# Expert 0's first layer on its first 256 rows moved among the last batch's routing, expert 1's first 256 rows in a pass of their own, column clears on GpSimd

## The chip, the cores and the metric

The kernel runs on one core of a Trainium2 chip, in one launch. The metric is the device time of that launch in microseconds (us): the median of several executions. One further execution, recorded by the hardware profiler, gives the trace from which rows are shown.

The engines are called as the profile calls them: PE is TensorE (matmuls; its weight loads are PEld), DVE is VectorE, ACT is ScalarE, POOL is GpSimd, SP is SyncE, which here only issues transfers.

## The reference

Three stages follow each other. All data are float32.

```python
# attention: 4 batches x 8 heads, 768 steps, heads of 48
for t in range(S):
    state = alpha[:, :, t, :, None] * state + einsum('bhd,bhe->bhde', k[:, :, t], v[:, :, t])
    y[:, :, t] = einsum('bhd,bhde->bhe', q[:, :, t], state)
# mixture of experts: N = 3072 rows of 384, 8 experts, hidden 1024, one expert per row
logits = (x / |x|) @ (emb / |emb|).T / tau
expert_idx = argmax(logits); gate_w = softmax(logits)[expert_idx]
out[mask_e] = gate_w * (relu(x[mask_e] @ w1[e]) @ w2[e])      # for each expert e
# a second feed-forward layer on all rows, hidden 2048
h = x @ w_in;  g = maximum(0.01 * h, h);  return g @ w_out
```

A row's expert is known only when its attention output is complete, so the experts' work starts after the routing.

## The kernel before, in words

**Precision.** A float32 product is made of three float16 matmuls: each operand is split into a high part and the rest (names end in h and l), and high x high, low x high and high x low are summed in one PSUM bank.

**Attention** runs over 16 units, four pairs of heads in each of four batches. Its operations are handed to `Plan` with an estimated duration, what they read and write, which PSUM bank they use, and a wish time `plan.at`. `Plan.order` makes a list schedule out of these, and the program is written in that order, one in-order queue for each engine. Where the plan expects gaps on PE, `keep_busy` puts matmuls without use (`pfill`, L357) into them.

**Routing.** `route(b)` follows each batch b: norms, logits, the arg max, the rank of each row within its expert (`ranks`) and its slot. Six indirect transfers on POOL (`scatter`, L667, one for each 128 rows) then write the rows of the batch, with their gate weight, into `bucket`, a table in DRAM with one region for each expert. Each scatter of a batch is issued behind the last.

**Early rows.** Of each expert's region the static part is CAP = 432 rows. `early_rows` fetches the first E0 = 256 rows of expert 0 (SP, L682, two blocks) once batch 2 is scattered, while the last batch is routed: these rows are the same whatever batch 3 adds. ACT scales them (L689), PE transposes them (L686), ACT writes the high part (L691) and DVE the rest (L692) of `xte`, which lies in the tile `shared`.

**The expert stage.** Its own `Plan` orders it. For expert e, `up(e, f, ...)` makes the eighth f of the hidden layer (9 matmuls: 3 products x 3 pieces of the contraction), with the relu into `held` by ACT (L1099) and the rest by DVE (L1100). `down(e, d, ...)` makes one third of the output columns (24 matmuls, L1118 to L1120), read by ACT (L1129) and DVE (L1130) into the column tiles `x2h` and `x2l`. Before the change, expert 0's `up` and `down` on the early 256 rows come first (f at wish times from -40, d from -30), then the rest of expert 0 (176 columns), then each expert with 432. Four PSUM banks `ps1` and four `ps2` are used in turn.

**Around it.** The weights of expert 0 are converted to float16 pairs during attention; those of expert e + 1, and pieces of the second layer's weights, during expert e (`fetch`, L1043; `piece`, L1048 on ACT and L1049 on DVE). Expert 1's tiles lie over tiles of the attention stage. `gather` fetches the other rows of experts 0 and 1 from `bucket` after the last scatter. `clear` (L1139) writes zeros on the columns behind each expert's static part, 12 pieces of 128 x 660, on ACT. After the routing the totals are counted by one matmul (L811) whose result gives the offsets of the experts, and `few`, which tells whether expert 0 had fewer than 256 rows after batch 2 (in which case a general pass at the end does its rows again).

The second feed-forward layer (L881 to L917) is PE work alone in its cost and is not touched, except that its weight pieces are spread otherwise over the experts.

## Time and profile before

| | |
|---|---|
| median of 3 runs | 738.17 us (738.13 to 738.73) |
| the profiled execution | 738.29 us |
| its span in the trace | 736.5 us |
| busy in the span: PE, DVE, ACT, POOL | 712.5, 583.4, 387.2, 100.6 us |
| mean granted clock of TensorE | 0.99 |

The span runs from the first to the last recorded instruction; the launch has 1.8 us around it. Busy shares are means over stages with different limits: attention and routing take the first 158 us or so, the experts and the second layer the rest, and a share tells nothing of which wait ends last in one stage. Granted clock 1.00 is TensorE's level of 2.4 GHz, 0.50 that of 1.2 GHz.

### The profile page before, as it was taken

To read this page: it belongs to the slowest core of one execution; us is meant where nothing else is said; L and a number is where in the kernel's file an instruction comes from. 1 tells how busy PE (TensorE), PEld (TensorE's weight loads), DVE (VectorE), ACT (ScalarE), POOL (GpSimd) and SP (SyncE) were. 2 spreads that over 40 slices of the span, in tenths; PEclk is the share of its full clock that TensorE was granted. 3 is DMA by queue.
4 is the path that set the end of the run, shared out by engine and by line. 5 is a ranking of instruction groups with operands and counts; after the bars stand their busy time and mean duration, and the time that the engine had idled before them with its cause. 6 is when DMAs were issued, how large, how long until landed. Compare 5 with 4: busy or idle time off the path is not lost.

```text
span 736.5 us, 16493 instructions
## 1 busy us (share of the span) xinstructions
PE 712.5 (97%) x6683; PEld 556.5 (76%) x6683; DVE 583.4 (79%) x1115; ACT 387.2 (53%) x758; POOL 100.6 (14%) x125
## 2 busy tenths in 40 slices
PE   7999989789999999999999999999999999999997
PEld 3778767558655555555588777999999999999996
DVE  7889889558887879988988888877878778768681
ACT  3354636339976677766755454443544544435440
POOL 7433635330000000000000110011010010110101
PEclk9999989899999999999999999999999999999999
DMA  8987935418999689886400000000000000000001
GB/s 297 304 239 234 293 128 172 142 66 189 269 251 239 196 196 236 200 232 181 144 1 1 13 16 19 1 23 22 2 22 2 23 24 1 23 23 2 24 1 46
DMA packets 62544, 82.77 MB, mean 112 GB/s; under 512 B 30840, under 2 KB 42496, under 8 KB 62464
## 3 DMA queue, kind: packets, MB, share of 16 engines
q1 hardware_dynamic: 58080, 71.13, 35.4%
q0 software_dynamic: 4224, 10.53, 4.0%
q8 instruction: 54, 0.88, 0.5%
q14 instruction: 26, 0.21, 0.1%
q10 hardware_dynamic: 160, 0.01, 0.0%
HBM read 62.09 MB, written 12.12 MB: 101 GB/s over the span
## 4 chain that ended last, share of the span: by engine, by line
PE 86%; DMA 5%; DVE 4%; ACT 1%; POOL 1%; issue 1%; another core or an unknown queue 1%; SPq 0%; POOLq 0%; DVEq 0%; ACTq 0%
PE ps L881 9%; PE ps L883 9%; PE ps L882 9%; PE ps L917 6%; PE ps L916 6%; PE ps L915 6%; PE ps L1094 5%; PE ps L1092 5%; PE ps L1093 5%; PE ps L1120 5%; PE ps L1119 5%; PE ps L1118 5%; PE py L516 2%; PE psc L456 2%; PE py L475 2%; DMA q<-in_qT 1%
## 5 line engine op out<-in xcount | busy, mean ns | idle before, releaser
L881 PE MATMUL ps<-x2h,wih 128*128 128x256 f16 x576 | 157.0, 273 | 0.0
L882 PE MATMUL ps<-x2l,wih 128*128 128x256 f16 x576 | 157.0, 273 | 0.0
L883 PE MATMUL ps<-x2h,wil 128*128 128x256 f16 x576 | 157.0, 273 | 0.0
L889 DVE TENSOR_TENSOR held<-ps,held 128x512 f32<-128x512 f32 x96 | 65.9, 686 | 51.0 <-ACT held L888 50.9
L949 POOL DMA_INDIRECT out<-wstage,tki x24 | 25.5, 1061 | 540.5 <-ACT wstage L1256 283.7
L888 ACT ACTIVATE held<-ps 128x512 f32<-128x512 f32 x96 | 57.3, 597 | 78.0 <-PE ps L883 61.6
L1118 PE MATMUL ps<-held,w2h 128*128 128x432 f16 (+2 forms) x216 | 70.1, 326 | 0.0
L1119 PE MATMUL ps<-held,w2h 128*128 128x432 f16 (+2 forms) x216 | 70.1, 326 | 0.0
L1120 PE MATMUL ps<-held,w2l 128*128 128x432 f16 (+2 forms) x216 | 70.1, 326 | 0.0
L1093 PE MATMUL ps<-xt,w1h 128*128 128x432 f16 (+1 forms) x192 | 63.6, 333 | 0.5 <-DVE xt L1018 0.5
L1092 PE MATMUL ps<-xt,w1h 128*128 128x432 f16 (+1 forms) x192 | 63.6, 333 | 0.4 <-ACT xt L1017 0.4
L1094 PE MATMUL ps<-xt,w1l 128*128 128x432 f16 (+1 forms) x192 | 63.6, 333 | 0.0
L881 PEld LDWEIGHTS <-wih 128*128 128x128 f16 x576 | 56.4, 98 | 6.8
L882 PEld LDWEIGHTS <-wih 128*128 128x128 f16 x576 | 56.4, 98 | 6.7
L883 PEld LDWEIGHTS <-wil 128*128 128x128 f16 x576 | 56.4, 98 | 6.5
L1100 DVE SCALAR_TENSOR_TENSOR held<-ps,held 128x432 f16<-128x432 f32 (+2 forms) x72 | 39.0, 552 | 11.8 <-ACT held L1099 9.8
L1099 ACT ACTIVATE held<-ps 128x432 f16<-128x432 f32 (+2 forms) x72 | 34.8, 488 | 23.9 <-PE ps L1094 23.4
L928 DVE SCALAR_TENSOR_TENSOR wstage<-ps,ms,wstage 128x192 f32<-128x192 f32 x80 | 31.9, 411 | 16.8 <-PE ps L917 16.7
L900 ACT ACTIVATE o1h<-held 128x256 f16<-128x256 f32 (+1 forms) x40 | 20.9, 523 | 30.7 <-DVE held L889 30.0
L900 ACT ACTIVATE o0h<-held 128x256 f16<-128x256 f32 (+1 forms) x40 | 20.9, 523 | 30.3 <-DVE held L889 29.7
L461 DVE TENSOR_TENSOR am<-psc,mask 128x768 f32<-128x768 f32 x32 | 30.0, 938 | 6.9 <-remote 3.7
L667 POOL DMA_INDIRECT bucket<-xb,slot x24 | 30.9, 1289 | 32.4 <-ACT shared L691 15.9
(282 smaller groups left out, 1869.6 us busy)
## 6 DMA issues: line engine op xcount, KB each, us to landing
wstage<-in_w SPq DMA_DIRECT2D x64, 384.0 KB
wstage<-in_w_in SPq DMA_DIRECT2D x16, 384.0 KB
wstage<-in_w_out SPq DMA_DIRECT2D x16, 384.0 KB
a<-in_aT SPq DMA_DIRECT2D x12, 387.5 KB
k<-in_kT SPq DMA_DIRECT2D x12, 384.0 KB
q<-in_qT SPq DMA_DIRECT2D x12, 384.0 KB
v<-in_v SPq DMA_DIRECT2D x8, 576.0 KB
xg<-bucket SPq DMA_DIRECT2D x6, 582.0 KB
```

The costliest lines, as they stand in the source:

```text
L881: nc.tensor.matmul(d, wih[:, k, fs], xs[0][k], start=k == 0, stop=False)
L882: nc.tensor.matmul(d, wih[:, k, fs], xs[1][k], start=False, stop=False)
L883: nc.tensor.matmul(d, wil[:, k, fs], xs[0][k], start=False, stop=k == KD - 1)
L888: add("ACT", 0.59, lambda: nc.scalar.activation(dst, src, AF.Copy, scale=0.01), [key], [("g", i)])
L889: add("DVE", 0.69, lambda: nc.vector.tensor_tensor(dst, src, dst, op=ALU.max), [key, ("g", i)], [("g", i)])
L915: nc.tensor.matmul(d, oh, wh, start=k == 0, stop=False)
L1092: nc.tensor.matmul(ps, w1h[:, f, k], xt[:, k], start=k == 0, stop=False)
L1093: nc.tensor.matmul(ps, w1h[:, f, k], xt[:, KD + k], start=False, stop=False)
L1094: nc.tensor.matmul(ps, w1l[:, f, k], xt[:, k], start=False, stop=k == KD - 1)
L1118: nc.tensor.matmul(ps, w2h[:, f, ds_], hh, start=f == 0, stop=False)
L1119: nc.tensor.matmul(ps, w2h[:, f, ds_], hl, start=False, stop=False)
L1120: nc.tensor.matmul(ps, w2l[:, f, ds_], hh, start=False, stop=f == NF1 - 1)
```

## The change

Four things are changed.

1. `early_rows(0)` asks for the row fetch after two of batch 2's scatters instead of six and transposes into the attention stage's banks `pkv` and `py`. A new `early_up` makes all of expert 0's first layer on the 256 rows within the attention plan, at wish time NU + 1.8, in three banks: `pkv` and the two halves of `py`, which is one tile. Its matmuls are L707 to L709, its relu L713 on ACT, its rest L714 on DVE. Fewer filler matmuls stand in that part of the program, and the call of `keep_busy` in `values` is left out.
2. `early_rows(1)` does the same fetch, scaling and transposing for expert 1's first 256 rows, into a weight stage tile. In the expert stage expert 0's `down` now comes first, then expert 1's `up` on those 256 columns, then the rest of expert 0; expert 1's later `up` has 176 columns. Four pieces of expert 1's first weight are fetched ahead of all others.
3. The 12 clears become memsets on POOL.
4. The pieces of the second layer's weights are spread 4, 3, 3, 3, 4, 5, 5, 5 over the experts instead of evenly, and some wish times move. `few` and the count are kept for two experts.

```diff
-        def early_rows():
-
-            u = (RU - 3) % 3
+        def early_rows(e):
+
+            u = (RU - 3 + e) % 3
             rows = (ta[u][:, :AUG], tq[u][:, :AUG])
             scaled = (ta[u][:, AUG:AUG + D], tk[u][:, :D])
             for n in range(E0 // P):
                 ts = slice(n * P, (n + 1) * P)
-                hi, lo = xte[:, :KD, ts], xte[:, KD:, ts]
                 held = ("a", "q")[n], u
-
-                def fetch(n=n, ts=ts):
-                    nc.sync.dma_start(rows[n], bucket[ts])
-
-                def turn(n=n):
+                bank, tp = (f"t{n}", ptr[n].rearrange("p k t -> p (k t)")) if e else (("kv", pkv), ("y0", py[:, 0]))[n]
+                own = ("tr", n) if e else ("eb", bank)
+                tp = tp[:, :KD * P].rearrange("p (k t) -> p k t", k=KD)
+
+                def fetch(n=n):
+                    nc.sync.dma_start(rows[n], bucket[e * NT + n * P:e * NT + (n + 1) * P])
+
+                def turn(n=n, tp=tp):
                     for k in range(KD):
-                        nc.tensor.transpose(ptr[n][:, k], scaled[n][:, k * P:(k + 1) * P], ident)
-
-                plan.add(Q_, 0.45, fetch, [("bucket", B - 2, c) for c in range(NC)], [held], size=(P * AUG * 4, 2.5))
-                plan.add(S_, 0.62, lambda n=n: nc.scalar.activation(scaled[n], rows[n][:, :D], AF.Copy, scale=rows[n][:, D:D + 1]), [held], [("early", n)] + [("k", u)] * n)
-                plan.add(T_, 0.45, turn, [("early", n)], [("tr", n)], pe=[f"t{n}"], flow=2 * KD * P)
-                plan.add(S_, 0.47, lambda n=n, hi=hi: nc.scalar.activation(hi, ptr[n][:, :KD], AF.Copy), [("tr", n)], [("xte", n)], ps=[f"t{n}"])
-                plan.add(V, 0.56, lambda n=n, hi=hi, lo=lo: nc.vector.scalar_tensor_tensor(lo, ptr[n][:, :KD], 1.0, hi, op0=ALU.mult, op1=ALU.subtract),
-                         [("tr", n), ("xte", n)], [("xtl", n)], ps=[f"t{n}"])
+                        nc.tensor.transpose(tp[:, k], scaled[n][:, k * P:(k + 1) * P], ident)
+
+                plan.add(Q_, 0.45, fetch, [("bucket", B - 2, c) for c in range(2)], [held], size=(P * AUG * 4, 1.0))
+                plan.add(S_, 0.62, lambda n=n: nc.scalar.activation(scaled[n], rows[n][:, :D], AF.Copy, scale=rows[n][:, D:D + 1]), [held], [("early", e, n)] + [("k", u)] * n)
+                plan.add(T_, 0.45, turn, [("early", e, n)], [own], pe=[bank], flow=2 * KD * P)
+                plan.add(S_, 0.47, lambda ts=ts, tp=tp: nc.scalar.activation(columns_of(e)[:, :KD, ts], tp, AF.Copy), [own], [("xte", e, n)] + [("wst", 0)] * e, ps=[bank])
+                plan.add(V, 0.56, lambda ts=ts, tp=tp: nc.vector.scalar_tensor_tensor(columns_of(e)[:, KD:, ts], tp, 1.0, columns_of(e)[:, :KD, ts], op0=ALU.mult, op1=ALU.subtract),
+                         [own, ("xte", e, n)], [("xtl", e, n)], ps=[bank])
+
+        def early_up():
+
+            (w1h, w1l), xt = shaped(w_first)[:2], columns_of(0)
+            late_rows = [(x, n, u, j) for x in ("pkh", "pqh") for n in range(2) for u in range(NR) for j in range(2)] + [("pen", 0, u, j) for u in range(NR) for j in range(2)]
+            y = [(f"y{i}", py[:, i]) for i in range(2)]
+            banks = [y[1], ("kv", pkv), y[0]] * 2 + [y[1], y[0]]
+            for f in range(NF1):
+                bank, ps = banks[f]
+                ps = ps[:, :E0]
+                hh, hl = (x[f][:, :E0] for x in hid)
+
+                def go(k, f=f, ps=ps):
+                    nc.tensor.matmul(ps, w1h[:, f, k], xt[:, k], start=k == 0, stop=False)
+                    nc.tensor.matmul(ps, w1h[:, f, k], xt[:, KD + k], start=False, stop=False)
+                    nc.tensor.matmul(ps, w1l[:, f, k], xt[:, k], start=False, stop=k == KD - 1)
+
+                for k in range(KD):
+                    plan.add(T_, 0.33, lambda k=k, go=go: go(k), [(x, f // 2) for x in ("whi", "wlo")] + [(x, 0, n) for x in ("xte", "xtl") for n in range(E0 // P)], [("eb", bank)], pe=[bank], flow=3 * E0)
+                plan.add(S_, 0.37, lambda ps=ps, hh=hh: nc.scalar.activation(hh, ps, AF.Relu), [("eb", bank)], [("hh", f)] + (late_rows if f > 2 else []), ps=[bank])
+                plan.add(V, 0.42, lambda ps=ps, hh=hh, hl=hl: nc.vector.scalar_tensor_tensor(hl, ps, 0.0, hh, op0=ALU.max, op1=ALU.subtract), [("eb", bank), ("hh", f)], [("hl", f)], ps=[bank])
...
+        first = []
+
+        def columns_of(e):
+
+            if e and not first:
+                first.append(stage())
+            return (first[0] if e else shared).bitcast(F16).rearrange("p (k t) -> p k t", k=2 * KD)
...
-            plan.at = NU + 1.7
-            early_rows()
+            plan.at = NU + 1.4
+            early_rows(0)
+            plan.at = NU + 1.8
+            early_up()
+            plan.at = NU + 1.9
+            early_rows(1)
...
+        turns = [1, 2, 3, 1]
+
         def fetch(src, at, cast=None):
-            m = len(fetched) % len(stages)
+            m = turns[len(fetched)] if len(fetched) < len(turns) else (len(fetched) - 2) % len(stages)
...
-                    plan.add(S_, 0.16 + w / 1200, lambda x=x: nc.scalar.activation(x, row0[:, 0:1].to_broadcast([P, w]), AF.Copy), ["bucket"], [("clear", n, d)], at=at)
+                    plan.add(G_, 1.0, lambda x=x: nc.gpsimd.memset(x, 0.0), ["bucket"], [("clear", n, d)], at=at)
...
-        plan.add("WAIT", 10.8, lambda: None, [], ["bucket"])
+        plan.add("WAIT", 8.0, lambda: None, [], ["bucket"])
         second = second_pieces()
-        per = -(-len(second) // E)
+        counts = (4, 3, 3, 3, 4, 5, 5, 5)
+        assert sum(counts) >= len(second)
         def pieces_of(e):
-            mine = [(begin(e) + 4.0 + 2.9 * j, weights, e + 1, j) for j in range(2 * KD * F1 // CH if e + 1 < E else 0)]
-            mine += [(begin(e) + 5.0 + 5.8 * j, *second[e * per + j]) for j in range(min(per, len(second) - e * per))]
+            mine = [(begin(e) + 4.0 + 2.9 * j - 8.0 * (1 <= e < 4), weights, e + 1, j) for j in range(2 * KD * F1 // CH if e + 1 < E else 0)]
...
+        mine = pieces_of(0)
+        add(mine[:4])
+        for d in range(KD):
+            down(0, d, d - 40.0, slice(0, E0))
         for f in range(NF1):
-            up(0, f, xte, f - 40.0, slice(0, E0), True)
-        for d in range(KD):
-            down(0, d, d - 30.0, slice(0, E0), True)
-        mine = pieces_of(0)
-        add(mine[:6])
+            up(1, f, columns_of(1), f - 35.0, slice(0, E0), True)
+        add(mine[4:6])
...
-            cols = slice(0 if e else E0, CAP)
+            cols = slice(0 if e >= EE else E0, CAP)
```

Lines have other numbers after the change: L569 became L567, L577 L575, L653 L651, L667 L665, L811 L844, L1092 L1130, L1118 L1156, L1043 L1078.

How the instructions stand on three engines (a name's number tells buffers apart; square brackets hold the semaphores for which an instruction waits, by the engine or DMA queue that raises them). PE, at the end of the routing, before: the transposes of the early rows, the count matmul, and the first matmul of expert 0's first layer.

```order
L686 MATMUL ptr_176<-ident,a_113 128x128 [waits Activation_49]
L686 MATMUL ptr_176<-ident,a_113 128x128 x2
L686 MATMUL ptr_177<-ident,k_119 128x128 [waits Activation_49]
L686 MATMUL ptr_177<-ident,k_119 128x128 x2
L811 LDWEIGHTS ones_75
L811 MATMUL pkv<-c_159,ones_75 128x9 [waits DVE_49]
L1092 LDWEIGHTS w1h [waits DVE_49,PE_49]
L1092 MATMUL ps_1878<-shared,w1h 128x256 [waits Activation_49]
```

PE, at the end of the routing, after: the last two groups of expert 0's first layer, the count matmul, and the first matmul of its second layer.

```order
L709 LDWEIGHTS w1l
L709 MATMUL py<-shared,w1l 128x256
L707 LDWEIGHTS w1h
L707 MATMUL py<-shared,w1h 128x256 [waits DVE_49]
L708 LDWEIGHTS w1h
L708 MATMUL py<-shared,w1h 128x256
L709 LDWEIGHTS w1l
L709 MATMUL py<-shared,w1l 128x256
L844 LDWEIGHTS ones_75
L844 MATMUL pkv<-c_159,ones_75 128x10 [waits DVE_49]
L1156 LDWEIGHTS w2h [waits DVE_49,PE_49]
L1156 MATMUL ps_1978<-held,w2h 128x256 [waits Activation_49]
```

The count matmul now stands behind all 24 groups of the first layer, and the group ahead of the last one is read by DVE before PE may go on. The group before that begins with such a wait for ACT.

ACT, in the last batch's routing, before: L569 and L577 are steps of the routing chain, L689 the scaling of the early rows.

```order
L552 ACTIVATE xb_170<-ptr_176 128x3x96 [waits PE_49]
L606 ACTIVATE late_164<-xb_170 128x6x96 [waits DVE_49,Activation_49]
L569 ACTIVATE lt_147<-ptr_176 128x384 [waits PE_49]
L577 ACTIVATE sm_150<-sm_150 128x6 [waits DVE_49]
L578 ACTIVATE sm_150<-sm_150 128x6 [waits Activation_49]
L689 ACTIVATE a_113<-a_113 128x384 [waits DMAHW2_49]
L653 ACTIVATE ex_156<-lg_152 128x48 [waits DVE_49]
L689 ACTIVATE k_119<-q_116 128x384 [waits DMAHW3_49]
```

The same place after the change; L567 and L575 are now those two steps.

```order
L689 ACTIVATE a_113<-a_113 128x384 [waits DMAHW0_49]
L525 ACTIVATE yT_144<-py 112x192 [waits DVE_49]
L550 ACTIVATE xb_170<-ptr_176 128x3x96 [waits PE_49]
L689 ACTIVATE k_119<-q_116 128x384 [waits DMAHW4_49,DMAHW1_49]
L691 ACTIVATE shared<-pkv 128x3x128 [waits PE_49]
L604 ACTIVATE late_164<-xb_170 128x6x96 [waits DVE_49,Activation_49]
L691 ACTIVATE shared<-py 128x3x128 [waits PE_49]
L567 ACTIVATE lt_147<-ptr_176 128x384
L689 ACTIVATE a_114<-a_114 128x384 [waits DMAHW5_49,DMAHW2_49]
L689 ACTIVATE k_120<-q_117 128x384 [waits DMAHW5_49,DMAHW3_49]
L575 ACTIVATE sm_150<-sm_150 128x6 [waits DVE_49]
L576 ACTIVATE sm_150<-sm_150 128x6 [waits Activation_49]
```

The scalings have moved from behind L577 to ahead of it, they have become four, and two L691 stand there too.

SP, where the row fetch is issued, before: the fetch of the rows (L682) waits for the six scatters of batch 2, and weight pieces (L1043) stand around it.

```order
L1043 DMA wstage<-in_w 128x768 [waits DMAHW5_49,DMAHW1_49,DVE_49]
L682 DMA a_113<-bucket 128x388 [waits DMASW5_49,DMASW4_49,DMASW6_49,DMASW3_49,DMASW7_49,DMASW2_49,DMAHW2_49,DMASW1_49,DMASW0_49]
L682 DMA q_116<-bucket 128x388 [waits DMAHW3_49]
L1043 DMA wstage<-in_w_in 128x768 [waits DMASW3_49,DMASW2_49,DMASW6_49,DMASW1_49,DMASW7_49,DMASW0_49,DMAHW2_49,DVE_49,DMAHW3_49,PE_49,Activation_49]
L1043 DMA wstage<-in_w 128x768 [waits DMAHW6_49,DVE_49]
```

After the change four row fetches stand together, the last with a wait for one more scatter (DMASW5), and the weight pieces (now L1078) that stood ahead have gone behind.

```order
L682 DMA a_113<-bucket 128x388 [waits DMASW5_49,DMASW4_49,DMASW6_49,DMASW3_49,DMASW7_49,DMASW2_49,DMAHW0_49,DMASW1_49,DMASW0_49]
L682 DMA q_116<-bucket 128x388 [waits DMAHW1_49]
L682 DMA a_114<-bucket 128x388 [waits DMAHW2_49]
L682 DMA q_117<-bucket 128x388 [waits DMAHW3_49,DMASW5_49]
L1078 DMA wstage<-in_w 128x768 [waits DMAHW4_49,DVE_49]
L1078 DMA wstage<-in_w 128x768 [waits DMAHW6_49,DMAHW5_49,DVE_49]
```

On POOL the sixth scatter of batch 2 now waits for the first three of these fetches.

## Rows read from the trace of the kernel before

**Rows 1.** Busy time by stretch: us, PE, PEld, DVE, ACT, POOL, clock, DMA.

```profile
178.00:731.00 553.00, 553.00 (x4749) 435.54 (x4746) 441.50 (x850) 302.90 (x532) 26.12 (x26) 1.00 0.31 82
```

**Rows 2.** Instructions of PE in order of time: start, duration, line, tiles, idle before.

```profile
157.92 0.17 PE L811 MATMUL pkv<-c,ones 128*128 128x9 f16 x1 [1.42 <-DVE c L809]
158.50 0.27 PE L1092 MATMUL ps<-shared,w1h 128*128 128x256 f16 x1 [0.41 <-DVE ohs L815]
...
159.37 0.27 PE L1094 MATMUL ps<-shared,w1l 128*128 128x256 f16 x1
...
161.34 0.27 PE L1094 MATMUL ps<-shared,w1l 128*128 128x256 f16 x1
...
167.78 0.27 PE L1118 MATMUL ps<-held,w2h 128*128 128x256 f16 x1
...
175.53 0.27 PE L1120 MATMUL ps<-held,w2l 128*128 128x256 f16 x1
...
176.89 0.24 PE L1092 MATMUL ps<-xt,w1h 128*128 128x176 f16 x1 [0.45 <-ACT xt L1017]
177.67 0.24 PE L1093 MATMUL ps<-xt,w1h 128*128 128x176 f16 x1 [0.55 <-DVE xt L1018]
...
178.35 0.24 PE L1093 MATMUL ps<-xt,w1h 128*128 128x176 f16 x1
```

**Rows 3.** The same, at the end of expert 1's first layer.

```profile
200.01 0.35 PE L1092 MATMUL ps<-xt,w1h 128*128 128x432 f16 x1
...
201.47 0.35 PE L1094 MATMUL ps<-xt,w1l 128*128 128x432 f16 x1
```

**Rows 4.** Instructions of ACT in order of time.

```profile
153.10 0.21 ACT L577 ACTIVATE sm<-sm 128x6 f32<-128x6 f32 x1 [1.19 <-DVE sm L576]
...
153.45 0.60 ACT L689 ACTIVATE a<-a 128x384 f32<-128x384 f32 x1
155.15 0.24 ACT L653 ACTIVATE ex<-lg 128x48 f32<-128x48 f32 x1 [1.10 <-DVE lg L652]
...
156.04 0.99 ACT L691 ACTIVATE shared<-ptr 128x384 f16<-128x384 f32 x2
161.07 0.66 ACT L1099 ACTIVATE held<-ps 128x256 f16<-128x256 f32 x2 [4.04 <-PE ps L1094]
163.68 0.39 ACT L1099 ACTIVATE held<-ps 128x256 f16<-128x256 f32 x1 [1.95 <-PE ps L1094]
165.91 0.94 ACT L1099 ACTIVATE held<-ps 128x256 f16<-128x256 f32 x3 [1.84 <-PE ps L1094]
...
175.84 0.38 ACT L1129 ACTIVATE x2h<-ps 128x256 f16<-128x256 f32 x1 [0.23 <-PE ps L1120]
```

**Rows 5.** Busy time by stretch, two more stretches.

```profile
140.80:147.70 6.90, 4.55 (x35) 3.27 (x35) 2.03 (x5) 1.89 (x4) 0.50 (x1) 0.51 0.31 104
148.69:153.10 4.41, 4.13 (x32) 1.93 (x32) 2.28 (x6) 2.19 (x6) 0.00 (x0) 1.00 0.01 4
```

**Rows 6.** Instructions of POOL in order of time.

```profile
140.34 0.96 POOL L667 DMA_INDIRECT bucket<-xb,slot  x1 [0.30 <-issue]
157.23 0.96 POOL L667 DMA_INDIRECT bucket<-xb,slot  x1 [15.93 <-ACT shared L691]
...
163.56 0.96 POOL L667 DMA_INDIRECT bucket<-xb,slot  x1 [0.30 <-issue]
```

**Rows 7.** Instructions of DVE in order of time.

```profile
158.13 0.16 DVE L812 TENSOR_SCALAR few<-pkv 128x1 f32<-128x1 f32 x1 [0.26 <-PE pkv L811]
...
171.01 0.42 DVE L1130 SCALAR_TENSOR_TENSOR x2l<-ps,x2h 128x256 f16<-128x256 f32 x1
```

**Rows 8.** The chain that ended last: start, us, what.

```profile
138.02 4.57 another core or an unknown queue
...
174.24 0.64 ACT x2l L1139
```

**Rows 9.** Groups of POOL by line and shape: busy us, mean ns.

```profile
L346 POOL MEMSET zero<- 128x388 f32 x1 | 0.4, 411 | 0.0
```

More of the change, by code (lines that the diff above doesn't have):

```diff
@@ L168 @@
 E0 = 2 * P
+EE = 2
 def to_f16_pair(nc, hi, lo, src, scale):
@@ L210, in body @@
     over = const.tile([P, 1 + 2 * OVB], I32, name="over")
-    seen, few = (const.tile([P, 1], F32, name=n) for n in ("seen", "few"))
+    seen, few = (const.tile([P, EE], F32, name=n) for n in ("seen", "few"))
     keep = ctx.enter_context(tc.tile_pool(name="keep", bufs=1))
@@ L650, in route @@
             if b == B - 2:
-                small(V, lambda: nc.vector.tensor_copy(seen, cnt[:, 0:1]), ["cnt"], ["seen"])
+                small(V, lambda: nc.vector.tensor_copy(seen, cnt[:, :EE]), ["cnt"], ["seen"])
             small(V, lambda: nc.vector.tensor_tensor(lg, lg, bcast(ls), op=ALU.mult), [key("lg"), key("ls")], [key("lg")])
@@ L950, in send @@
                                      in_=rows, in_offset=None, bounds_check=NT - 1, oob_is_err=False)
-    first = [stage() for _ in range(4)]
     both = ExitStack()
@@ L960, in body @@
         xts = [mxp.tile([P, 2 * KD, CAP], F16, name=f"xt{i}", bufs=1) for i in range(2)]
+        first += [stage() for _ in range(3)]
         stages = first + [wst2.tile([P, CH], F32, name="wstage")]
@@ L986, in gather @@
             if e < 2:
-                for n in range(0 if e else E0 // P, NB):
+                for n in range(E0 // P, NB):
                     plan.add(Q_, 0.45, lambda n=n: block(n), ["bucket"], [("xg", e), ("row", e, n)], size=(P * AUG * 4, 2.5), at=float(e))
@@ L1082, in step, with parts @@
         def step(n):
-            return max(0.1, n * 0.1828 / CAP)
+            return n * 0.1828 / CAP + 0.0005
+        def parts(cols):
+            return [p for p in range(2) if (cols.start < E0, cols.stop > E0)[p]]
         def up(e, f, xt, at, cols, early=False):
@@ L1094, in go @@
                     nc.tensor.matmul(ps, w1l[:, f, k], xt[:, k], start=False, stop=k == KD - 1)
-            rows = [("sg", i) for i in range(2)] if early else [("xt", e % 2, b, i) for b in range(cols.start // P, NB) for i in range(2)]
-            key = ("h", f, early)
+            rows = [("wst", 0)] if early else [("xt", e % 2, b, i) for b in range(cols.start // P, NB) for i in range(2)]
+            keys = [[("h", f, p, i) for p in parts(cols)] for i in range(2)]
             plan.add(T_, 9 * step(n), go, [("w", e % 2, 0, f // 2, i) for i in range(2)] + rows, [("ps1", f % 4)], at=at)
-            plan.add(S_, 0.16 + n / 1200, lambda: nc.scalar.activation(hh, ps, AF.Relu), [("ps1", f % 4)], [(*key, 0)], at=at)
-            plan.add(V, 0.155 + n / 960, lambda: nc.vector.scalar_tensor_tensor(hl, ps, 0.0, hh, op0=ALU.max, op1=ALU.subtract), [("ps1", f % 4), (*key, 0)], [(*key, 1)], at=at)
+            plan.add(S_, 0.16 + n / 1200, lambda: nc.scalar.activation(hh, ps, AF.Relu), [("ps1", f % 4)], keys[0], at=at)
+            plan.add(V, 0.155 + n / 960, lambda: nc.vector.scalar_tensor_tensor(hl, ps, 0.0, hh, op0=ALU.max, op1=ALU.subtract), [("ps1", f % 4)] + keys[0], keys[1], at=at)
         offset = {}
@@ L1122, in down @@
             for f in range(NF1):
-                plan.add(T_, 3 * step(n), lambda f=f: go(f), [("w", e % 2, 1, f // 2, i) for i in range(2)] + [("h", f, early, i) for i in range(2)], [("ps2", b)], at=at + 0.05 * f)
+                plan.add(T_, 3 * step(n), lambda f=f: go(f), [("w", e % 2, 1, f // 2, i) for i in range(2)] + [("h", f, p, i) for p in parts(cols) for i in range(2)], [("ps2", b)], at=at + 0.05 * f)
             def place(i):
@@ L1179, in body @@
             for d in range(KD):
-                down(e, d, begin(e) + 13.2 + 4.4 * d - 12.0, cols)
+                down(e, d, begin(e) + 13.2 + 4.4 * d - 12.0, slice(0 if e else E0, CAP))
             if e == 0:
```

30 lines of the change are left out of this document (15 added, 15 removed).

## The prediction, made before the changed kernel was run

> **What bounds the kernel now.** I read the busy time by stretch first. From 178 us to 731 us TensorE (PE) is busy for all of the 553.00 us at granted clock 1.00 [rows 1]: nothing in the MoE and second-FFN stages waits long enough to show. The total is therefore set by two things: when this unbroken stretch begins and how much matmul work lies in it. A change earns time only if it lets that work begin sooner or makes it less.
>
> Then I read PE's order of time at the seam [rows 2]. The routing ends at 157.92 (the count matmul L811). Expert 0's first layer on its first 256 rows begins at 158.50, its second layer (L1118) at 167.78 and ends at 175.53, and the remaining 176 columns begin at 176.89 and 177.67 after two small waits. The second layer's 72 matmuls take (175.53 - 167.78) / 71 = 0.109 us each, 7.86 us in all. The first layer has 72 of the same width and takes 9.28 us, so 1.4 us of it are waits.
>
> **One number carries the change.** After it PE does: expert 0's first layer (earlier), its second layer, expert 1's first layer on 256 columns, then the rest as before. Expert 1's 72 early matmuls are work moved within the full stretch. They cost 72 x 0.109 = 7.86 us there and later make 72 matmuls of 432 columns into 72 of 176. Those take (201.47 - 200.01) / 8 = 0.1825 us [rows 3] and (178.35 - 177.67) / 9 = 0.0756 us [rows 2], so 7.70 us are saved: a loss of 0.16. So, but for the waits just before 177.67, the total moves by (start of expert 0's second layer after the change) - 167.78 + 0.16. Were the first layer wholly hidden in the routing, the second layer would start near 160 and 7 us be won. The question is only where that start, call it S, comes to lie.
>
> **Routing, with more in it.** Four row scalings L689 of 0.60 us each [rows 4] and two L691 now stand ahead of L575 on ScalarE (ACT); before, all of these stood behind it (it was L577, at 153.10). Two L691 take 0.99 together [rows 4]. That is 3.4 us more in a stretch from 148.69 to 153.10 of which ACT was busy 2.19 of 4.41 [rows 5]. 2.2 + 3.4 = 5.6 is 1.2 us more than 4.41, so the chain behind L575 moves by about 1.1 us (one scaling may fit ahead of 148.69). Bounds: 0 if the scalings all find gaps; +2 if expert 1's second row block, which is fetched only after the sixth scatter of batch 2, lands late and holds the in-order ACT queue ahead of L575. I take 1.1, since the sum of the rows gives it. With it L653 moves from 155.15 to 156.3 [rows 4], and batch 3's scatters, 157.23 to 164.52 before [rows 6], to about 158.4 to 165.7.
>
> **The early first layer, hop by hop.** The 72 matmuls come as 24 groups of three. By the order of the program 8 groups are free of new waits and go among the routing. Of the other 16, ten begin with a wait for ACT or VectorE (DVE) to have read the bank, since two of its three banks are one tile (py): a write into one half waits for the read of the other. One such hop is: from the first to the last matmul of a group 0.22; from there to the answer 0.31 (175.53 to 175.84, [rows 2, 4]); the answer itself, 0.39 on ACT [rows 4] or 0.42 on DVE [rows 7]; 0.05 back. That is 0.97 to 1.00 us for 0.33 us of matmul. Laid out: ACT's first read begins behind L653 at 156.6, group 9 starts at 157.25, group 10 at 158.8 (two reads and the transposes stand before it), group 12 at 159.8. Six groups run through to 161.8. Then come groups 18, 19, 20, 21 at 162.1, 163.1, 164.1, 165.05, group 23 at 166.35 and group 24 at 167.35. Its ACT read ends at 168.3, its DVE read at 168.75. Only then follow the casts, the count matmul (169.0), and, as from 157.92 to 158.50 before, some 0.45 us until the second layer's first matmul: **S = 169.45**. Against 167.78 that is **+1.67**.
>
> **Late answers while scatters run.** Before the change ACT reads the first of these sums at 161.07, though its last matmul starts at 159.37; it reads the third at 163.68, after 161.34; the next at 165.91 [rows 2, 4]. With the usual 0.31 they would have come 1.4 and 2.0 us sooner. All of it lies while GpSimd issues scatters, and I have no cause for it. Four banks hid most of that before. The new chain has no spare bank, so a late answer stops PE. Bounds: nothing (the count's answer at 158.13, 0.21 us after its matmul, came promptly during the first scatter [rows 2, 6, 7]); or answers at the spacing 161.07, 163.68, 165.91, with which only three answers come by 166 where my layout has six: +3.2 us. I take the middle, **+1.6**.
>
> **The edits with one answer.** The 12 clears leave ACT (one of them, 0.64 us, stands in the chain that leads to the wait ending at 177.67 [rows 2, 8]). That wait may shrink by up to 1.0 us; I take **-0.5**. On GpSimd one clear costs about 0.41 x 660 / 388 = 0.70 us by the memset of [rows 9], 8.4 us for twelve from about 168, and expert 1's second layer, which writes over those columns, lies behind 201.47 [rows 3]: no cost; if that cover were gone, 8.4 us. Expert 1's four w1 pieces are on SyncE's queue behind the row fetches, and their casts behind the last scatter: from about 168, four at 0.95 us, done by 172.5; PE wants them at S + 7.9 = 177.3. No cost, with 4.8 us to spare. The regrouped second-FFN weights shift DVE and ACT work by a few us; from 178 to 731 they are busy 441.50 and 302.90 of 553 us [rows 1], and PE does not wait: nothing, up to 1 us of loss.
>
> **Sum.** 1.67 + 0.16 + 1.6 - 0.5 = +2.9 us. The profiled execution took 738.29 us (span 736.5 plus 1.8 around it), 0.12 above the median of 738.17, so the forecast is 738.17 + 2.9 = **741.1 us**. A difference under 0.2%, 1.5 us, I count as no change.
>
> **Rivals.**
>
> *The answers come promptly.* Then 1.6 falls away: 739.5, on the edge of no change. For it speaks the prompt answer at 158.13; against it the three late ones in the same batch's scatters.
>
> *The stall upstream goes (faster).* The chain has 4.57 us, from 138.02 to 142.61, that it gives to "another core or an unknown queue" [rows 8]. It ends after six scatters of batch 2 in a row, the last issued at 140.34 [rows 6]; the clock that follows is 0.51 over 140.8 to 147.7, the half level of 1.2 GHz, in which half of the 4.55 us of PE work, 2.27, is lost [rows 5]. Five scatters now run in a row and the sixth waits for row fetches. If the stall ends with the last scatter of the run, it ends 1.26 us sooner; if it dissolves with the half clock behind it, 4.57 + 2.27 - 0.3 = 6.5 us come back: 741.1 - 6.5 = 734.6. It decides from 2.9 + 1.5 = 4.4 us on. Against: nothing removes the scatters, and the sixth now falls among the routing's own answers.
>
> *The clock falls in the hop chain.* The clock was seen at half after the chain had stood for 4.57 us [rows 5, 8]; the new chain has PE at work a third of the time for some ten us. If it falls as it did at 140.8, a like stretch costs its 2.27 us again: 743.4, and up to 746 with the late answers at their bound. Against: the idle stretches of 1.42 and 0.41 us before 157.92 and 158.50 [rows 2] are followed by matmuls at the full 0.109 us. The Trainium skill (TensorE: Matmul & The Clock Gate, section "Why this matters for your kernels") says to leave no idle gaps between bursts of matmuls, because TensorE then falls back to its lower clock, and so speaks against this interleaving. By it, this rival's 743.4 would be the likeliest time; this trace agrees after the 4.57 us stall (clock 0.51), and no row of it shows a chain of short gaps like the new one.
>
> *The early work is hidden after all.* If the ACT and DVE reads overlap better than the waits say and S falls to 165, the change would win 2.6 to 3: 735.4. It needs four hops fewer than the program has; I give it little.
>
> **Chances.** The forecast, answers more or less late (739.8 to 743): 0.36. Prompt answers (739 to 740): 0.18, half of it slower by over 1.5 us, half not. The lower clock, or the late answers at their bound (743 to 746): 0.14. The upstream stall shorter by over 4.4 us: 0.18 (733 to 736.5). The early work hidden: 0.06 (735 to 736.5). Five scatters in a row end the stall 1.26 us sooner and the answers come promptly, so that losses and gains nearly cancel (736.8 to 739.6): 0.08, no change. So slower 0.36 + 0.09 + 0.14 = 0.59, same 0.09 + 0.08 = 0.17, faster 0.18 + 0.06 = 0.24. The range reaches from inside the stall's case to inside the clock's, 734.8 to 745, and leaves out about 0.1 at each end. The likeliest case alone spans 739.8 to 743.
>
> **What the profile after will show.** Right: PE's groups of three L707 to L709 about 1 us apart after the ranks, releaser alternately ACT and DVE on held; the first L1156 at 169 to 172; no PE waits beyond it except before the 176-column part; clock 1.00 there. The routing's L575 about 1.1 us later than L577 was, at equal times upstream. Wrong, if the first L1156 starts before 166, if the stall before 142.61 is gone, or if PE waits for w1 or for the columns of experts 1 and 2 after 178.

## The result, and the profile after

The changed kernel takes 742.37 us (739.88 to 743.61, 7 runs) against 738.31 us (736.49 to 738.75, 7 runs) before: ratio 1.0056, 95% interval 1.0039 to 1.0072. It is slower, by about 4 us. The forecast was 741.1 with the range 734.8 to 745. The execution from which the trace after comes took 743.61 us (span 741.7), at the upper end of its runs and 5.3 us above the profiled execution of before.

First PE in order of time, at the seam. Line numbers are those of after: L707 to L709 are the early first layer, L844 the count matmul, L1156 the first matmul of expert 0's second layer.

```profile
160.55 0.27 PE L709 MATMUL py<-shared,w1l 128*128 128x256 f16 x1
...
161.29 0.27 PE L707 MATMUL py<-shared,w1h 128*128 128x256 f16 x1
...
162.35 0.27 PE L707 MATMUL py<-shared,w1h 128*128 128x256 f16 x1 [0.57 <-DVE held L714]
...
163.31 0.27 PE L707 MATMUL py<-shared,w1h 128*128 128x256 f16 x1 [0.47 <-issue]
...
164.38 0.27 PE L707 MATMUL py<-shared,w1h 128*128 128x256 f16 x1 [0.58 <-issue]
...
165.92 0.37 PE L707 MATMUL py<-shared,w1h 128*128 128x256 f16 x1 [0.47 <-ACT held L713]
...
167.30 0.37 PE L707 MATMUL py<-shared,w1h 128*128 128x256 f16 x1 [0.59 <-DVE held L714]
...
169.18 0.17 PE L844 MATMUL pkv<-c,ones 128*128 128x10 f16 x1 [1.08 <-DVE c L842]
169.76 0.37 PE L1156 MATMUL ps<-held,w2h 128*128 128x256 f16 x1 [0.42 <-DVE ohs L848]
...
174.84 0.38 PE L1156 MATMUL ps<-held,w2h 128*128 128x256 f16 x1
...
175.16 0.27 PE L1158 MATMUL ps<-held,w2l 128*128 128x256 f16 x1
```

From 161.29 on the steps are 0.96 to 1.54 us long, and five of them begin with a wait of 0.5 to 0.6 us. A group is 0.33 us of matmul at the full clock; the step from 164.38 to 165.92 holds two groups, and from there on the lower clock stretches them. The second layer starts at 169.76, where it started at 167.78 [rows 2]. Its matmuls take 0.37 to 0.42 us until 174.84 and 0.27 us from 175.16 on. The busy time by stretch shows why (the number before the last two is the granted clock):

```profile
162.00:164.00 2.00, 0.98 (x6) 0.58 (x6) 0.72 (x3) 0.38 (x1) 1.70 (x2) 1.00 0.53 199
164.00:166.00 2.00, 1.14 (x7) 0.76 (x7) 0.33 (x1) 0.38 (x1) 0.99 (x2) 0.70 0.36 134
166.00:168.00 2.00, 1.41 (x6) 0.72 (x6) 0.42 (x1) 0.00 (x0) 0.00 (x0) 0.50 0.19 69
168.00:170.00 2.00, 0.50 (x4) 0.21 (x3) 1.11 (x8) 0.38 (x1) 0.00 (x0) 0.50 0.00 0
170.00:172.00 2.00, 2.00 (x11) 1.40 (x10) 0.99 (x7) 0.00 (x0) 0.51 (x1) 0.50 0.04 8
```

PE had worked for half of the stretch from 162 to 164, in short pieces, when the clock fell to its 1.2 GHz level; it stayed there until the second layer had run for 5 us without a gap. From 169.93 to 174.84, 23 matmuls take 0.2135 us each instead of 0.109: 2.4 us lost there, and about 0.1 more in the step at either end.

ACT in the same part of the program:

```profile
141.55 0.49 ACT L525 ACTIVATE yT<-py 112x384 f32<-112x384 f32 x1 [3.19 <-remote]
...
148.14 0.49 ACT L525 ACTIVATE yT<-py 112x384 f32<-112x384 f32 x1 [2.61 <-PE py L475]
...
153.39 0.61 ACT L689 ACTIVATE k<-q 128x384 f32<-128x384 f32 x1 [0.70 <-DMA q<-bucket]
153.91 0.19 ACT L575 ACTIVATE sm<-sm 128x6 f32<-128x6 f32 x1
...
160.86 0.38 ACT L713 ACTIVATE held<-py 128x256 f16<-128x256 f32 x1 [2.53 <-PE py L709]
...
172.56 2.31 ACT L1083 ACTIVATE w1h<-wstage 128x768 f16<-128x768 f32 x3 [4.05 <-POOL x2h L1177]
```

The read at 160.86 answers the matmul of 160.55 after 0.31 us, as fast as ever: no answer is late here. What waits after the seam is little (all waits of PE from 172 us on):

```profile
PE ps L1131 <- DVE xt L1051: 0.4, 1, 0.4
PE ps L1045 <- DVE held L1138: 0.4, 1, 0.4
PE ps L1130 <- ACT xt L1050: 0.4, 1, 0.4
PE ps L914 <- DVE held L922: 0.3, 1, 0.3
```

That is 1.5 us, of which 1.0 us stood there before too [rows 2]. So the 5.3 us of this trace are: second layer later, 1.98; its lower clock, 2.5; waits, 0.5; the split of expert 1's layer, 0.16 by the working of the prediction. They sum to 5.1. The same working, against the profiled execution of before, fits two traces shown below: with fillers 1.74 + 0.16 + 0.5 = 2.4 us where 2.43 were measured (740.72), and with all mends -3.98 + 0.16 + 0.5 = -3.3 where -3.34 were measured (734.95). So the time follows the start of the second layer and its clock; what makes that start late is a second question.

### The profile page after: what moved, and what is told of

Its sections match the earlier page's. It is cut to its first block, busy times and chain, and to the rows that moved or that the text cites. A ratio compares the mean times of both kernels' runs of the same rounds, so it can differ in the third digit from the quotient of the medians.

```text
span 741.7 us, 16661 instructions
## 1 busy us (share of the span) xinstructions
PE 716.5 (97%) x6752; PEld 563.5 (76%) x6752; DVE 584.7 (79%) x1124; ACT 381.1 (51%) x756; POOL 108.6 (15%) x137
## 5 line engine op out<-in xcount | busy, mean ns | idle before, releaser
L1156 PE MATMUL ps<-held,w2h 128*128 128x432 f16 (+2 forms) x216 | 71.4, 332 | 0.4 <-DVE ohs L848 0.4
L1157 PE MATMUL ps<-held,w2h 128*128 128x432 f16 (+2 forms) x216 | 71.3, 331 | 0.0
L1131 PE MATMUL ps<-xt,w1h 128*128 128x432 f16 (+1 forms) x192 | 60.8, 319 | 0.4 <-DVE xt L1051 0.4
L1130 PE MATMUL ps<-xt,w1h 128*128 128x432 f16 (+1 forms) x192 | 60.8, 319 | 0.4 <-ACT xt L1050 0.4
L1132 PE MATMUL ps<-xt,w1l 128*128 128x432 f16 (+1 forms) x192 | 60.8, 319 | 0.0
L1137 ACT ACTIVATE held<-ps 128x432 f16<-128x432 f32 (+2 forms) x72 | 33.1, 462 | 22.9 <-PE ps L1132 22.1
L1138 DVE SCALAR_TENSOR_TENSOR held<-ps,held 128x432 f16<-128x432 f32 (+2 forms) x72 | 37.2, 523 | 7.6 <-ACT held L1137 7.3
L665 POOL DMA_INDIRECT bucket<-xb,slot x24 | 30.9, 1288 | 33.0 <-DVE slot L656 10.5
L938 DVE TENSOR_TENSOR st<-held 128x256 f32<-128x256 f32 x80 | 33.7, 422 | 1.4
```

Source lines behind the costliest of these rows:

```text
L1130: nc.tensor.matmul(ps, w1h[:, f, k], xt[:, k], start=k == 0, stop=False)
L1131: nc.tensor.matmul(ps, w1h[:, f, k], xt[:, KD + k], start=False, stop=False)
L1132: nc.tensor.matmul(ps, w1l[:, f, k], xt[:, k], start=False, stop=k == KD - 1)
L1156: nc.tensor.matmul(ps, w2h[:, f, ds_], hh, start=f == 0, stop=False)
L1157: nc.tensor.matmul(ps, w2h[:, f, ds_], hl, start=False, stop=False)
```

## The experiments

Three sets of four kernels ran, each on a chip of its own, beside the kernel before, which took 738.7, 730.8 and 739.6 us (medians of 19, 22 and 31 runs). Ratios are to the kernel before of the same set, and kernels of different sets are compared by these ratios alone. Theory A: the shared tile py makes the hop chain, and its gaps cost the clock. B: the longer routing costs. C: something downstream does. D came after the second set.

**py as two tiles.**

```diff
-        py = pa.tile([P, 2, 512], F32, name="py")
+        py = [pa.tile([P, 512], F32, name=f"py{i}") for i in range(2)]
```

> The changed kernel with the tile py made of two tiles of one bank each, and nothing else. Theory A (the waits between the halves of py make the hop chain, and its gaps let the clock fall): most of the ten group waits go, the groups L707 to L709 run nearly back to back after the ranks, expert 0's second layer starts at 164 to 166 instead of 169.8, the clock stays 1.00, total 735 to 737. Theory B (the routing with its four row scalings ahead of L575 is what costs): the start moves by less than 1 us and the total stays at 741 to 743.

Measured: 741.54 us, ratio 1.0041 (1.0026 to 1.0056). Both theories miss. The chain of hops is gone, as A says, but the rows show two other waits in its place. First PE (line numbers are one higher here):

```profile
162.64 0.27 PE L710 MATMUL py<-shared,w1l 128*128 128x256 f16 x1
166.19 0.17 PE L845 MATMUL pkv<-c,ones 128*128 128x10 f16 x1 [3.28 <-DVE c L843]
166.78 0.37 PE L1157 MATMUL ps<-held,w2h 128*128 128x256 f16 x1 [0.42 <-DVE ohs L849]
```

And ACT of the same trace:

```profile
151.87 0.61 ACT L690 ACTIVATE k<-q 128x384 f32<-128x384 f32 x1 [3.01 <-DMA q<-bucket]
...
163.67 0.38 ACT L714 ACTIVATE held<-py 128x256 f16<-128x256 f32 x1 [2.41 <-PE py L710]
165.15 0.38 ACT L714 ACTIVATE held<-py 128x256 f16<-128x256 f32 x1 [1.09 <-remote]
```

The matmuls of the last groups start back to back until 162.64, 5 us sooner than in the changed kernel (167.68). Then the last answers are late after all, at 163.67 and 165.15, and the count can follow only at 166.19. And ACT stands 3.01 us for expert 1's second row block ahead of L576: the routing had arrived that much sooner. The clock fell behind that wait (matmuls of 0.42 us from 156.50 on) and again in the wait of 3.28 us.

The routing was there sooner because the attention's last unit, which uses py too, ended sooner. Its last read by ACT in this trace, and in that of the fillers (same set):

```profile
145.30 0.33 ACT L526 ACTIVATE yT<-py 112x192 f32<-112x192 f32 x1 [0.85 <-DVE yT L528]
148.10 0.33 ACT L525 ACTIVATE yT<-py 112x192 f32<-112x192 f32 x1
```

That is 2.8 us, and the second layer starts 2.7 us sooner than with the fillers (166.78 against 169.52). So by these traces the hops that went at the seam gave nothing on balance; the late answers and the longer wait took their place.

**Fillers that hold the clock.**

```diff
+                    if f > 4 and (f, k) not in ((5, 0), (5, 1), (6, 1)):
+                        keep_busy("f")
+                        keep_busy("f")
...
+            for _ in range(4):
+                keep_busy("f")
             nc.tensor.matmul(tot, ones16, tc16, start=True, stop=True)
```

> The changed kernel with two filler matmuls of 512 columns behind seven of the last groups of the early first layer and four ahead of the count matmul; no wait is taken away. Theory A1 (the fall of the clock at 164.8 is a cost of its own, about 2.5 us, in most runs): the start of expert 0's second layer stays within 169 to 170.3, the clock stays 1.00 there, total 739.5 to 740.8 and with less spread. Theory A2 (the late start alone explains the loss): the total stays at 741.5 to 743.

Measured: 741.0 us, ratio 1.0031 (1.0016 to 1.0045). PE at the start of the second layer (L1161 here):

```profile
169.52 0.27 PE L1161 MATMUL ps<-held,w2h 128*128 128x256 f16 x1 [0.45 <-DVE ohs L853]
```

And the busy time of two stretches, with the granted clock:

```profile
164.00:166.00 2.00, 1.51 (x10) 0.97 (x10) 0.42 (x1) 0.22 (x1) 0.02 (x1) 1.00 0.26 99
170.00:172.00 2.00, 2.00 (x21) 1.79 (x19) 0.81 (x5) 0.00 (x0) 0.76 (x2) 1.00 0.03 8
```

The second layer starts where it did without fillers (169.52), the clock stays at 1.00, and the ratio is 0.0025 lower, 1.8 us. With A1 the start and the clock were right and the time 0.2 us above its range; the intervals touch, so the size is rough. As far as that goes, the fall of the clock is a cost of its own, and the late start alone leaves 0.3%.

**The first layer back in the expert stage.**

```diff
-            early_up()
...
+        for f in range(NF1):
+            up(0, f, columns_of(0), f - 50.0, slice(0, E0), True)
```

> The changed kernel without early_up: expert 0's first layer on its 256 rows back in the expert stage ahead of its second layer, all else as changed (both early row fetches, scalings ahead of L575, expert 1's early pass, clears on GpSimd, weight counts). Theory A: the total comes back to before's, 737.5 to 739.3. Theory B (the routing is what costs): 740 or more. Theory C (the later weight casts, the blocked SyncE queue and the regrouped pieces cost downstream): 739.5 to 741 with waits of PE past 180.

Measured: 746.78 us, ratio 1.012 (1.0096 to 1.0144), slower than all three theories say. It does not separate them, because it makes a wait of its own, PE's longest:

```profile
PE ps L1128 <- DVE held L1136: 4.6, 1, 4.6
```

ACT shows what the reads of these sums stand behind:

```profile
165.81 0.84 ACT L1081 ACTIVATE w1h<-wstage 128x768 f16<-128x768 f32 x1 [11.26 <-DMA bucket<-xb,slot]
166.56 0.36 ACT L1135 ACTIVATE held<-ps 128x256 f16<-128x256 f32 x1
```

The cast of expert 1's weight, which must wait for the last scatter, now stands ahead of all reads of expert 0's sums on the in-order ACT queue, and PE stops when its four banks are full. In the kernel before, six of the eight reads stood ahead of that cast. So the rest of the change was not tested on its own.

**The clears back on ACT.**

```diff
-                    plan.add(G_, 1.0, lambda x=x: nc.gpsimd.memset(x, 0.0), ["bucket"], ...
+                    plan.add(S_, 0.16 + w / 1200, lambda x=x: nc.scalar.activation(x, row0[:, 0:1].to_broadcast([P, w]), AF.Copy), ["bucket"], ...
```

> The changed kernel with the 12 clears back on ScalarE. Theory A: no measurable difference from the changed kernel, 741.5 to 743.5. Rival (the clears had been in the way on ScalarE and their move is worth something): 743.5 or more.

Measured: 746.75 us, ratio 1.0108 (1.008 to 1.0135); the rival holds. PE's longest waits past 172:

```profile
PE ps L1130 <- DMA xt<-xs: 1.9, 1, 1.9
PE ps L1130 <- ACT xt L1050: 0.8, 1, 0.8
```

ACT's work between the late seam and expert 1's rows has become tight: with the clears among it, the scaling of the rows ends 0.75 us later than in the changed kernel (187.91 against 187.16), and their transposed transfer is issued at 188.47 instead of 186.96, behind fetches of weights on SP: too late for expert 1's 176 columns. GpSimd is the right place for the clears in the changed kernel, and worth about 0.5% there.

**Expert 1's scalings behind the routing.**

```diff
- ... AF.Copy, scale=rows[n][:, D:D + 1]), [held], [("early", e, n)] + [("k", u)] * n)
+ ... AF.Copy, scale=rows[n][:, D:D + 1]), [held] + [("ex", 1)] * e, [("early", e, n)] + [("k", u)] * n)
```

> The changed kernel with the two row scalings L689 of expert 1's rows held back until the routing's exponential L651 has been issued, so that they no longer stand ahead of L575 on ScalarE. Theory B (part of the loss is the routing behind these scalings): L575 comes 0.7 to 1.5 us earlier against L525 and the total falls by 0.5 to 1.5 us against the changed kernel, to 741 to 742. Rival (the hop chain sets the end whatever the routing does): no difference; 742 to 743.

Measured: 738.89 us (4 runs, 735.85 to 742.18) beside 730.77: ratio 1.0112 (1.0071 to 1.0154). The set had no run of the changed kernel, so B is not decided by it. In this set the kernel before itself was 8 us faster, and the trace of the kernel before with two tiles, of the same set (below), shows what is missing.

**Both edits, and with six fillers ahead of the count matmul.**

> Both edits: py as two tiles, and the scalings of expert 1's rows behind L651. In the run with two tiles alone ScalarE waited 3.0 us for expert 1's second row block ahead of L575, and PE then stood 2.35 us and fell to the lower clock at 155.4. Theory A with B (each edit had been hidden by the other's wait): the routing comes about 3 us earlier, expert 0's second layer starts at 163 to 165, total 736.5 to 739, 2.5 us or more below either edit alone. Rival (late answers during the scatters take it back): 740 or more.

> The same with six filler matmuls ahead of the count matmul. If the clock falls in the idle stretch there without them: 1 to 2.5 us below the kernel without fillers, 735.5 to 738. If the clock had not fallen: the same time, or up to 0.5 us more.

Measured: 736.37 us, ratio 1.006 (1.0037 to 1.0084), and 733.84 us, ratio 1.004 (1.0023 to 1.0057). Both lie below the expected ranges, by 0.1 and 1.7 us, but only because the whole set is faster; against the kernel before both lose. The fillers took 2.5 us off the median and 0.0020 off the ratio, and the intervals overlap. What they win at the count is not shown: there the granted clock is 1.00 in both traces, and the lower clock lies upstream, behind the wait shown next (0.50 from 144 to 156 without fillers, from 146 to 148 with them). ACT, with the fillers:

```profile
144.47 0.61 ACT L690 ACTIVATE a<-a 128x384 f32<-128x384 f32 x1 [2.91 <-DMA a<-bucket]
144.99 0.31 ACT L526 ACTIVATE yT<-py 112x192 f32<-112x192 f32 x1
```

The scaling of expert 0's rows waits 2.91 us for their fetch and holds up the last unit's own copy L526 behind it. The second layer of this kernel starts at 162.14.

**The kernel before with py as two tiles.**

> The kernel before with py as two tiles and nothing of the change. If the two tiles shorten the attention's last units as the run with two tiles alone suggests (the step L567 there at 147.9, 3.8 us earlier than in the changed kernel's trace): 735 to 737. If not: 738 to 739.

Measured: 729.64 us, ratio 0.999 (0.9976 to 1.0004): no difference that shows (the microseconds expected for either case miss, because the set is faster). Its trace has no upstream stall. ACT's reads in the last unit:

```profile
136.89 0.49 ACT L528 ACTIVATE yT<-py 112x384 f32<-112x384 f32 x1 [1.17 <-PE py L517]
...
140.01 0.49 ACT L528 ACTIVATE yT<-py 112x384 f32<-112x384 f32 x1 [0.29 <-PE py L517]
```

And the busy time of that stretch:

```profile
138.00:144.00 6.00, 5.92 (x64) 3.32 (x61) 2.44 (x5) 3.39 (x7) 1.92 (x2) 1.00 0.41 140
```

Here the six scatters run as in [rows 6], and yet L528 answers after 0.29 us where the chain of the first trace had stood 4.57 us [rows 8], and the clock does not fall. In all traces of the first and third set a wait of ACT in the last unit ends 1.0 to 1.3 us after the last scatter of the run has ended (before the change at 142.61, behind 141.30); in none of the second set does it. So the stall does not come with the scatters alone; it comes and goes with the set, or with the chip, which these runs do not tell apart. What raises it stays open. Theory D follows: where it is absent, the early row fetch is late for ACT.

**The changed kernel again.**

> The changed kernel itself, to have it and its trace beside the next three on one chip. In the runs of the second set the kernel before took 730.8 us instead of 738.7, and a trace of a kernel of that set shows no stall of 4.6 us in the attention's last unit and no lower clock after it. Theory D (the upstream stall, where it occurs, hides the early row fetch; without it ScalarE waits for that fetch in the middle of the last unit, ahead of L525): if the kernel before is again near 731, the changed kernel is 1.0% or more slower, with ScalarE's L689 waiting 2 to 3 us for the fetch; if it is near 738.5, 0.3 to 0.7% slower with no such wait.

Measured: 743.86 us beside 739.64, ratio 1.0061 (1.0039 to 1.0082), the second of D's two cases: its L689 does not wait for the fetch. In this trace the chain of hops, with the same waits of 0.5 to 0.6 us, keeps the clock at 1.00 until 170; only behind the waits of 1.08 and 0.42 us at the count is it 0.54 (170 to 172). The changed kernel itself was not run where the stall is absent, so D's first case was not seen on it, only on kernels built from it.

**All four scalings held back.**

```diff
- ... [held], [("early", e, n)] + [("k", u)] * n)
+ ... [held] + [("ex", 1) if e else ("lt", 0)], [("early", e, n)] + [("k", u)] * n)
```

> The changed kernel with all four row scalings held back: expert 0's behind L567, expert 1's behind L651. Theory D: if the kernel before is near 731, 2 to 4 us faster than the changed kernel on the same chip; if it is near 738.5, 0 to 1.5 us faster. Rival (the hop chain alone sets the end): the same time as the changed kernel on either chip.

Measured: 743.56 us, ratio 1.0054 (1.0036 to 1.0073), the same as the changed kernel, which both theories allow. In its trace L651 runs at 154.14 and the second layer starts at 169.58; in the changed kernel's of this set, at 156.77 and 170.40. The 2.6 us are not the scalings' alone: the plan also ordered the last unit otherwise, and ACT's last read of it comes 3.5 us sooner (145.16 against 148.68). Of them 0.8 are left behind the hop chain, and these go to the clock, which is at half from 164 on:

```profile
164.00:166.00 2.00, 1.53 (x8) 0.95 (x7) 0.00 (x0) 0.38 (x1) 0.00 (x0) 0.50 0.26 99
172.00:174.00 2.00, 2.00 (x11) 1.35 (x10) 0.75 (x1) 1.62 (x3) 2.00 (x4) 0.50 0.00 0
```

**All mends together:** two tiles, four scalings back (both as above), and

```diff
+            for _ in range(6):
+                keep_busy("f")
             nc.tensor.matmul(tot, ones16, tc16, start=True, stop=True)
```

> All mends together: py as two tiles, the four scalings held back, six filler matmuls ahead of the count matmul. Theories A, B and D together: 4 us or more below the changed kernel on the same chip, and within 0.3% of the kernel before or below it. If it is still 0.4% or more above the kernel before, something else in the change costs, and the trace should show PE standing there.

Measured: 736.82 us, ratio 0.9967 (0.995 to 0.9985): 7 us below the changed kernel of the same set and 0.3% faster than the kernel before, as expected. The trace is of the fastest of its ten executions (734.95; the slowest took 739.83). PE at the seam (L847 is the count, L1159 the second layer):

```profile
163.21 0.17 PE L847 MATMUL pkv<-c,ones 128*128 128x10 f16 x1 [1.62 <-DVE c L843]
163.80 0.27 PE L1159 MATMUL ps<-held,w2h 128*128 128x256 f16 x1 [0.42 <-DVE ohs L851]
```

And the granted clock behind it:

```profile
164.00:166.00 2.00, 2.00 (x21) 1.78 (x20) 1.03 (x7) 0.00 (x0) 0.47 (x1) 1.00 0.03 8
```

The second layer starts 6.6 us sooner than in the changed kernel of this set (170.40). But most of that is won ahead of the seam. ACT's last reads of the attention's last unit, first in the changed kernel, then here (two reads in one row):

```profile
148.68 0.33 ACT L525 ACTIVATE yT<-py 112x192 f32<-112x192 f32 x1
142.93 0.87 ACT L526 ACTIVATE yT<-py 112x384 f32<-112x384 f32 x2
```

The unit ends some 5 us sooner, with another order of its work, and the clock is 1.00 there, where it is 0.50 from 144 to 152 in the changed kernel. The sum of the mends is shown; which of them gives what is not, nor that the gain comes from the seam, for which they were made.

**The kernel before with only the clears on GpSimd** (the plus line of the edit of the clears, in the kernel before).

> The kernel before with only the 12 clears moved to GpSimd. My term: 0 to 1.0 us faster, most likely 0.5. Rival (memsets on GpSimd slow VectorE's work in the weights and PE comes to wait): 0.5 us or more slower.

Measured: 740.58 us, ratio 1.0011 (1.0000 to 1.0021): no gain, at most a small loss. PE's waits past 172:

```profile
PE ps L1092 <- ACT xt L1017: 0.9, 1, 0.9
PE ps L1119 <- DVE held L1100: 0.5, 1, 0.5
PE ps L1093 <- DVE xt L1018: 0.5, 1, 0.5
```

The wait that was to shrink by 0.5 us, 0.45 and 0.55 in [rows 2], is 0.9 and 0.5 here. The trace has a second cost that the clears do not explain. PE at the count, and the busy time behind it, with the granted clock:

```profile
159.44 0.17 PE L811 MATMUL pkv<-c,ones 128*128 128x9 f16 x1 [1.42 <-DVE c L809]
160.00:161.00 1.00, 0.98 (x5) 0.71 (x6) 0.83 (x6) 0.00 (x0) 0.96 (x1) 0.51 0.53 199
```

This is the idle stretch of [rows 2], with the same waits of 1.42 and 0.42 us, and here the matmuls behind it run at the half clock until 163.4; in [rows 2] they run at the full one.

## Why the prediction was right, and where it was not

**The accounting held.** The time follows the start of expert 0's second layer: forecast 169.45 without late answers, measured 169.76. Nothing moved downstream of it could make this good, and PE's further waits came to 1.5 us. That the start fits so well is in part luck: the chain ran 0.8 us ahead of the layout (group 18 at 161.29 instead of 162.1), and at the lower clock it lost that lead (group 24 at 167.30 instead of 167.35).

**Routing: right.** From L525 to L575 it took 5.77 us (148.14 to 153.91) where L527 to L577 had taken 4.41 (148.69 to 153.10 [rows 4, 5]): 1.36 us more, against 1.1. The wait of 0.70 us for expert 1's second block, a bound of the forecast, is in it. The stall ahead of it ended 1.06 us sooner (141.55), close to the 1.26 of a rival, but did not go. That this routing sets the end is not shown: with all scalings held back the routing was 2.6 us sooner and the time the same.

**Hops: right.** One took 0.96 to 1.07 us at the full clock, against 0.97 to 1.00. That the waits between py's halves make them is shown by the kernel with two tiles, where the last groups run back to back. Not all ten came to a hop: five waits took 0.47 to 0.59 us, the others 0.3 us or less. And that the hops are what makes the end late is argued only: without them other waits took their place.

**Late answers, +1.6: wrong in this trace.** They measure 0. One of the three rows on which the term rested was misread. ACT's read at 161.07 stands, in program order, behind a load of `offi` into registers, which the profile does not list and which waits for DVE's L818. And the bound of +3.2 took rows for answers: the rows at 161.07 and 165.91 hold two and three reads, so that six had come by 167, not three by 166. In the kernel before with two tiles DVE writes `offi` (L819) until 151.69 and the first read comes at 152.81, 1.1 us later, with prompt reads behind it; before the change the distance is the same. The other two rows were late, and such answers came in the run with two tiles (163.67, 165.15), but not in the changed kernel's. They keep company with the stall: the last of them ends 1.4 us after the last scatter in both traces (165.91 behind 164.52, 165.15 behind 163.80), and in the second set's trace of the kernel before with two tiles all reads during the scatters are prompt. Their cause is as open as the stall's.

**The clock, left out of the sum: wrong.** The rival had the mechanism and the price, 2.27 us, and got a chance of only 0.14, shared with another case. It measured 2.5 us, and PE was at the lower clock in this trace, in that with the clears on ACT, in that with the scalings back and, for a shorter time, in the changed kernel of the third set. The rule of the Trainium skill that the prediction weighed (TensorE: Matmul & The Clock Gate, "Why this matters for your kernels") is written for long idle gaps between bursts, which the prediction does not say; here the clock fell in a chain of gaps of 0.5 to 0.6 us between short groups, much shorter ones. The idle stretches of 1.42 and 0.41 us were no argument against it: in the trace of the kernel before with the clears moved, the same stretches are followed by the half clock. Nor does one trace tell that it will fall: the same chain kept the full clock in the third set's. So of the signs, "clock 1.00 there" was wrong, and this term, put at nothing, is the one that the forecast lacked.

**The clears, -0.5: wrong.** Alone they win nothing that shows, though the lower clock in that trace may hide part of it. In the changed kernel, which makes ACT's work tight, moving them back costs 0.5%.

So the total came near by two errors that cancel: +1.6 that was not there, and 2.5 that was left out.

**What was not foreseen:** the register load moved too. `offi` is ready at 171.2 after the change, and ACT's casts of expert 1's weights start at 172.56 instead of the assumed 168; SP stands behind them, its four fetches of w1 pieces taking from 150.20 to 174.76. The first three pieces were cast by 176.1, the fourth, which the last part of the layer uses, only by 182.5. PE began that layer at 180.19, 2.9 us later than forecast, and did not wait for a weight; that it began so late is the clock's doing, so the assumption on the casts happened not to matter.

## What to carry to other kernels

Work that is moved into another stage's gaps takes on that stage's buffers: count the banks that are tiles of their own, because in this program a write to one half of a shared tile waited for the read of the other, and five such waits of 0.5 to 0.6 us stood in a row. A chain of short waits on TensorE can also cost the clock of the full stretch behind it, 2.5 us here; fillers held it at the same start of the layer. Before you credit a mend at one place, compare the traces ahead of it: most of what two tiles and all mends together gained had been gained an attention unit earlier. On an in-order queue, place an operation that depends on a transfer behind the work that does not, whatever a planner's landing time says.

## What the runs showed of the hardware

- In every trace of the first and third set a wait of ScalarE in the last attention unit ended 1.0 to 1.3 us after the last indirect scatter of the run; in the second set, where the kernel before takes 730.8 us, none did. 8 us, twice the size of the change, depend on the set or its chip.
- What a broken stretch does to TensorE's clock was not the same from one execution to the next: behind idle stretches of 1.42 and 0.41 us it was 1.00 in one trace and, behind the same, 0.51 in another; a chain of waits of 0.5 to 0.6 us brought it to 0.50 in one trace of the changed kernel and left it at 1.00 in the other.
- Twelve memsets of 128 x 660 float32 on GpSimd took 0.65 us each, against 0.74 on ScalarE, and VectorE's casts beside them kept their pace (0.96 us each, 0.95 before the change).
- ScalarE's first operation behind a load of a register from SBUF came 1.1 us after VectorE had written the value in two traces (151.69 to 152.81, 159.96 to 161.07), and 1.36 us after it where waits for the scatters stood between too (171.20 to 172.56).
